# Conversion work queued behind a slot's other work on ScalarE, and w_out split by the second block

## The chip, the cores and the metric

The kernel runs on one core of one Trainium2 chip. The metric is the device time of one execution in microseconds; the time of a kernel is the median of several runs. TensorE (PE) does the matmuls, VectorE (DVE), ScalarE (ACT) and GpSimd (POOL) the element work, and SyncE (SP) only issues DMAs. Each engine takes its instructions in the order in which the program lists them, so an instruction that waits holds up all that stands behind it on its engine.

## The reference

Pooled attention feeds a dense layer pair, and its result a routed layer with eight experts, of which each token takes one:

```python
k_p = k.reshape(B, H, Sp, pool, D).mean(axis=3)          # B=8, H=8, Sp=72, pool=8, D=64
v_p = v.reshape(B, H, Sp, pool, D).mean(axis=3)
attn = softmax(scale * np.matmul(q, k_p.transpose(0, 1, 3, 2)))
x = np.matmul(attn, v_p)                                   # 4608 tokens x 512
h = x @ w_in                                               # 512 x 2048
g = np.where(h >= 1, h, np.where(h <= -1, 0.0, (h + 1) ** 2 / 4))
x = g @ w_out                                              # 2048 x 512
expert = argmax(x @ w_gate, axis=1)                        # 8 experts
out = gate_w * (np.maximum(x @ w1[expert], 0.0) @ w2[expert])
```

All data is float32.

## The kernel before

The 4608 tokens are 36 tiles of 128, in ten blocks (3, then 4 each, then 3 and 2 tiles). Each block runs 16 steps, one for each chunk of 128 hidden units. In step m, `f1` multiplies chunk m+2 of w_in with the block's x (12 matmuls), and `f2` multiplies chunk m's activations with chunk m of w_out (3 matmuls a tile). Every float32 product is made of three matmuls on operands split into a high and a low part; the high part is a ScalarE copy, the low part a subtraction (`low_part`, line 266, on GpSimd for weights).

Between `f1` and `f2`, and again after `f2`, stands a slot: an even one and an odd one in each step. Slots carry the attention of the next block's tiles as units: `u_qt` (transposes q, line 384 and its ScalarE copy 386), `u_sc_all` (scores, line 327; reductions 334 and 336 on VectorE; the exponential, line 341, on ScalarE), `u_turn_p` and `u_place_p` (probabilities turned through DRAM: transposes 414 and 416, store to `p_d` line 417, load into `PT` line 423), `u_pv` (line 443, copies 449 and 450). Units come round about every three steps in the first block.

The first block (`j == 0`, here from about 30 to 150 us) also prepares the weights. Each weight chunk is loaded raw (`load_raw`, SP queue) and goes through `tick`, one tick a slot: `convert_a` is two ScalarE passes (lines 545 and 549, the second writes `SGN`, a part of tile `WG`); `convert_b` queues two VectorE passes in `pend` (line 557, which reads the raw words and `SGN` and writes a PSUM bank, and line 560, which finishes the chunk `dst`); `mix` takes work from `pend`. Two ticks later `convert_c` makes the high part on ScalarE (line 571) and the low part on GpSimd (line 266). Chunks of w_in stay in `W`. Chunks of w_out go into one of four slots of `WO`, and the first block also stores their high and low parts to `wo_d` in DRAM (line 574, 512 KB a chunk), from where all later blocks load them (`load_out`, line 611, ScalarE queue).

`f1`'s own element work is a chain over two engines: line 626 (VectorE), 627 (ScalarE), 631 (VectorE, in `larger`), 632 (ScalarE, `larger`), 266 (VectorE, `lower`). `larger`, `lower` and some parts of units go into the list `later`, which `flush` empties once in a slot, in the order in which they were put in. Each `f1` writes PSUM bank 0 or 1 by turns. The score and transpose units share two more banks in the first block.

The lines that set the order in a slot of the first block are `tick()`, then the units, then `flush()`; `tick(late)` either calls `convert_a` and `convert_b` at once or appends them to `later`. After a block, `route_steps` finds each token's expert in small steps, one or two a slot, with a number of pauses between (`wait`).

Of the kernel before, what the change touches and what calls it, by code (L numbers as in the profile page):

```python
# [8 lines left out]
F32 = mybir.dt.float32  # L9
# [4 lines left out]
ACTF = mybir.ActivationFunctionType  # L14
# [10 lines left out]
def attention_ffn_routed_experts_kernel(  # L25
# [12 lines left out]
    nc = tc.nc  # L38
    B, H, S, D = q.shape
    NT, DM = out.shape  # L40
# [5 lines left out]
    KF = DFF // 128  # L46
# [16 lines left out]
    NB = len(blocks)  # L63
# [7 lines left out]
    dram = ctx.enter_context(tc.tile_pool(name="dram", bufs=1, space=bass.MemoryType.DRAM))  # L71

    wo_d = dram.tile([KF, 128, 2, DM], F32R, name="wo_d")
    yrow_d = dram.tile([NT + 128, ROW], F32, name="yrow_d")
    perm_d = dram.tile([128 * NE * NTILE, 1], I32, name="perm_d")
    perm_t = perm_d.rearrange("(p e r) o -> p (e r o)", p=128, e=NE)
# [7 lines left out]
    def r32(ap):  # L84
        return ap.bitcast(F32)
# [3 lines left out]
    WO = sb.tile([128, 4, 2, DM], F32R, name="WO")  # L89
# [17 lines left out]
    def fx(o, n):  # L107
        return FX[:, o:o + n]
# [24 lines left out]
    WOF = [fx(512 + 512 * i, 512) for i in range(4)]  # L133
# [5 lines left out]
    def wi(m, lo, c):  # L139
        o = m * 1024 + lo * 512 + c * 128  # L140
        return W[:, o:o + 128]

    def wi4(m, lo):
        o = m * 1024 + lo * 512
        return W[:, o:o + 512]
# [119 lines left out]
    def low_part(lo, x, hi, eng=nc.gpsimd):  # L265
        eng.tensor_tensor(out=lo, in0=x, in1=r32(hi), op=ALU.subtract)  # L266
# [3 lines left out]
    def mix(n=1):  # L270
        for _ in range(min(n, len(pend))):
            pend.popleft()()
# [3 lines left out]
    def flush():  # L276
        for _ in range(len(later)):
            later.popleft()()
# [257 lines left out]
    def cvt_dst(i):  # L536
        m, o = order[i]
        return (WOF[m % 4] if o else DFI[m % 3]), RB[i % NRB].rearrange(
            "p a (x w) -> p a x w", w=2)
# [23 lines left out]
    def convert_ab(i):  # L563
        convert_a(i)
        convert_b(i)

    def convert_c(i):
        m, o = order[i]
        dst, _ = cvt_dst(i)
        hi, lo = (WO[:, m % 4, 0], WO[:, m % 4, 1]) if o else (wi4(m, 0), wi4(m, 1))  # L570
        nc.scalar.activation(out=hi, in_=dst, func=ACTF.Copy)  # L571
        low_part(lo, dst, hi)
        if o:
            nc.sync.dma_start(out=r32(wo_d[m]), in_=r32(WO[:, m % 4]))


    FIRST, MORE = AHEAD + 2, 1
# [12 lines left out]
    def more_raw(i):  # L590
        if i < len(order) and order[i]:
            load_raw(*order[i], i % NRB)

    def tick(late=False):

        n = ticks[0]
        mix(4)
        if n > 0:
            more_raw(n - 1 + NRB)
        if 0 <= n - 2 < len(order) and n != 3:  # L600
            convert_c(n - 2)
        if n < len(order):
            if late:
                later.append(lambda: convert_ab(n))
            else:
                convert_ab(n)
        ticks[0] += 1

    def load_out(g):

        nc.scalar.dma_start(out=r32(WO[:, g % 4]), in_=r32(wo_d[g % KF]))

    def f1(j, m):
        g = j * KF + m
        n = blocks[j][1] * 128
        o = ps[m % 2][:, 0:n]
        for c in range(KD):
            xh, xl = XT[:, j % 2, 0, c, 0:n], XT[:, j % 2, 1, c, 0:n]
            nc.tensor.matmul(o, wi(m, 0, c), xh, start=(c == 0), stop=False)  # L619
            nc.tensor.matmul(o, wi(m, 0, c), xl, start=False, stop=False)  # L620
            nc.tensor.matmul(o, wi(m, 1, c), xh, start=False, stop=(c == KD - 1))  # L621
        r = (JK if j == 0 and m % 2 else FR)[:, 0:n]
        gh, gl = FG[:, g % (AHEAD + 1), 0, 0:n], FG[:, g % (AHEAD + 1), 1, 0:n]


        nc.vector.tensor_scalar(r, o, -1.0, 1.0, op0=ALU.max, op1=ALU.min)  # L626
        nc.scalar.activation(out=r, in_=r, func=ACTF.Square, scale=0.5, bias=half)  # L627
        mix()

        def larger():  # L630
            nc.vector.tensor_tensor(out=o, in0=r, in1=o, op=ALU.max)  # L631
            nc.scalar.activation(out=gh, in_=o, func=ACTF.Copy)  # L632
            if KF <= g + 1 < len(steps):
                load_out(g + 1)
            later.append(lower)

        def lower():
            low_part(gl, o, gh, nc.vector)
        later.append(larger)
# [26 lines left out]
    def route_steps(j, bk):  # L666
# [22 lines left out]
            nc.tensor.matmul(pb[:, 0:n * 32], PICK4, LT[:, 0:n * 32], start=True, stop=True)  # L689
            V.transpose(out=LGT[:, 0:n].rearrange("p t x -> p (t x)"), in_=pb[:, 0:n * 32])  # L690

        wait = 2 if j < NB - 2 else 1
        for t in range(n):
            st.append(lambda t=t: turn(t))
            st.extend([pause] * wait)
# [107 lines left out]
    def pick_first():  # L803
        V = nc.vector
        cnt = CB[:, 0]
        mx, mn = MX4[:, 0], MN4[:, 0]
        g = G1[:, 0]
        V.tensor_reduce(out=mx, in_=cnt, axis=AX.X, op=ALU.max)
        V.tensor_scalar(g, cnt, mx, None, op0=ALU.is_equal)
        V.scalar_tensor_tensor(out=g, in0=g, scalar=-16.0, in1=iota4[:, 0], op0=ALU.mult,  # L810
                               op1=ALU.add)
        V.tensor_reduce(out=mn, in_=g, axis=AX.X, op=ALU.min)
        V.tensor_scalar(FST, g, mn, None, op0=ALU.is_equal)
        V.tensor_scalar(FSI, mn, 16.0, None, op0=ALU.add)
        V.tensor_copy(FSR, FSI)

        V.tensor_scalar(POS0, FSI, -float(CAP), -float(EARLY * 128), op0=ALU.mult, op1=ALU.add)
        for t in range(LN):
            V.tensor_scalar(IDF[:, t:t + 1], pcol, float((blocks[-1][0] + t) * 128 - NT), None,
                            op0=ALU.add)  # L820
# [4 lines left out]
    def fetch_first(dst, t0, n):  # L825
        r = nc.values_load(FSR[0:1, 0:1], engines=[SP], min_val=0, max_val=NE - 1)
        nc.sync.dma_start(out=dst, in_=tiles_of[:, bass.ds(r, 1), t0:t0 + n].rearrange(
            "p o r -> p (o r)"))
# [5 lines left out]
    def load_first(i):  # L834
        if not first:
            first.append(nc.values_load(FSR[0:1, 0:1], engines=[ACT], min_val=0, max_val=NE - 1))
        src = (w1, w2)[i // 4][bass.ds(first[0], 1)].rearrange("o (c p) f -> p (o c) f", p=128)

        if i < 4:
            nc.scalar.dma_start(out=ST1[:, i:i + 1], in_=src[:, i:i + 1])  # L840
        else:
            nc.scalar.dma_start(out=ST2[:, 2 * i - 8:2 * i - 6], in_=src[:, 2 * i - 8:2 * i - 6])
# [129 lines left out]
    def q_gather(qn, i):  # L972
        gather(XG[i], q_ids(qn, i), qn == 0)
# [158 lines left out]
    with tc.manual_schedule():  # L1132
# [9 lines left out]
        def run_units(n):  # L1142
            for _ in range(n):
                units.popleft()[1]()
            if qloads:
                qloads.popleft()()
# [64 lines left out]
        steps = [(j, m) for j in range(NB) for m in range(KF)]  # L1211
# [14 lines left out]
        def slot(j, s):  # L1226

            want = min(state["units"], -(-(s + 1) * state["units"] // (22 if j == NB - 2 else 29 - 2 * AHEAD + 2)))
            wide[0] = False
            if j == 0:  # L1230
                for _ in range(min(1, PER[s // 2]) if s % 2 == 0 else PER[s // 2] - 1):
                    tick()
            run_units(want - state["done"])
            state["done"] = max(want, state["done"])
            flush()
            if j == 0 and kv:
                kv.popleft()()
            for _ in range(2 if j >= NB - 2 else 0 if wide[0] else 1 + s % 2):
                if todo:
                    todo.popleft()()  # L1240
            if j == PICK + 2 and s == 0:
                pick_first()
            for i in range(8):
                if 32 * (j - NB + 2) + s == LF[i]:
                    load_first(i)
            if j == NB - 2:

                if s == 1:
                    fetch_first(IDA, 0, EARLY)
                if s == 9:  # L1250
                    for i in range(EARLY):
                        q_gather(0, i)
            if j == NB - 1:
                if s == 3:
                    nc.gpsimd.iota(IO, pattern=[[1, 128]], base=0, channel_multiplier=0,
                                   allow_small_or_imprecise_dtypes=True)
                if s == 17:
                    fetch_first(IDQ, EARLY, 4 * NQ)
                if s == 27:
                    nc.vector.tensor_copy(IDMF, IDQ)  # L1260
                if s in CV1:
                    cvt1(CV1.index(s))
                if s in QT0:
                    q_tx(0, QT0.index(s))
                if s in (25, 27):
                    cvt2(0, (s - 25) // 2)

        for m in range(AHEAD):
            f1(0, m)
            flush()  # L1270
            while ticks[0] < CAHEAD + 2 + m:
                tick()
                flush()
        for g, (j, m) in enumerate(steps):
            if m == 0:
# [222 lines left out]
```

## Time and profile before

| | us |
|---|---|
| median of 3 runs | 1396.14 (1395.46 to 1397.46) |
| the profiled execution | 1394.67 |
| its span in the trace | 1393.0 |
| PE busy | 1353.9 (97%) |
| DVE / ACT / POOL busy | 762.4 / 433.3 / 355.5 |

The time of the profiled execution is 1.67 us more than its span, and 1.47 us less than the median. A busy PE says little by itself; what matters is where it stands idle, and behind whom.

### The profile page before, as it was taken

The page shows a single profiled execution, that of the slowest core. Times are in us where ns is not written, and L with a number is a line of the kernel's source. Part 1 is how long each engine was busy: PE and PEld are TensorE (multiplying, and loading weights), DVE is VectorE, ACT ScalarE, POOL GpSimd, SP SyncE. Part 2 cuts the span into 40 slices and gives each one's busy share as a digit, 9 for nine tenths or more (in the row PEclk, how much of TensorE's full clock was granted, in tenths as well). Part 3 has the DMA queues.
Part 4 walks back from the last instruction along what each step waited for, and adds up shares of the span by engine and source line. Part 5 has one row for each costly group of instructions (what it writes and reads, how often), then busy time and mean ns, then how long its engine had stood idle before and what let it go on. Part 6 is the DMA issues. An engine that isn't in the chain of part 4 may idle for free. (4 is left out here: it accounts for less than half of the span.)

```text
span 1393.0 us, 22129 instructions
## 1 busy us (share of the span) xinstructions
PE 1353.9 (97%) x8114; PEld 1111.7 (80%) x8114; DVE 762.4 (55%) x1539; ACT 433.3 (31%) x730; POOL 355.5 (26%) x517
## 2 busy tenths in 40 slices
PE   7788999999999999999999999999999999999998
PEld 6666778888778788788788788889878888888886
DVE  5698566656666675566666556455532323323426
ACT  5667232222222222222222233343121111111335
POOL 4475636004304203313310011021231211111211
PEclk9899999999999999999999999999999999999999
DMA  9986656546637555555453344572543223331235
GB/s 235 287 274 221 186 144 193 144 123 176 179 116 197 149 161 155 159 166 150 148 158 111 111 142 146 187 264 79 182 137 107 92 72 109 104 107 59 86 125 188
DMA packets 170702, 213.48 MB, mean 153 GB/s; under 512 B 83431, under 2 KB 114439, under 8 KB 170568
## 3 DMA queue, kind: packets, MB, share of 16 engines
q1 hardware_dynamic: 135992, 102.29, 25.7%
q10 hardware_dynamic: 26784, 88.16, 18.9%
q0 software_dynamic: 7792, 21.35, 4.7%
q8 instruction: 71, 1.16, 0.4%
q14 instruction: 63, 0.52, 0.1%
HBM read 188.30 MB, written 47.03 MB: 169 GB/s over the span
## 5 line engine op out<-in xcount | busy, mean ns | idle before, releaser
L619 PE MATMUL ps<-XT,W 128*128 128x512 f32 (+2 forms) x640 | 243.3, 380 | 5.3 <-ACT W L571 2.4
L621 PE MATMUL ps<-XT,W 128*128 128x512 f32 (+2 forms) x640 | 237.6, 371 | 2.2 <-POOL W L266 2.2
L620 PE MATMUL ps<-XT,W 128*128 128x512 f32 (+2 forms) x640 | 237.6, 371 | 0.5 <-DVE XT L450 0.5
L647 PE MATMUL ps<-WO,FG 128*128 128x512 f32 x576 | 231.2, 401 | 1.0 <-ACT Y L656 1.0
L648 PE MATMUL ps<-WO,FG 128*128 128x512 f32 x576 | 225.9, 392 | 0.0
L649 PE MATMUL ps<-WO,FG 128*128 128x512 f32 x576 | 225.3, 391 | 0.0
L627 ACT ACTIVATE FX<-FX,half 128x512 f32<-128x512 f32 (+2 forms) x152 | 104.0, 684 | 379.7 <-DVE FX L626 357.9
L626 DVE TENSOR_SCALAR FX<-ps 128x512 f32<-128x512 f32 (+2 forms) x152 | 96.9, 638 | 122.0 <-PE ps L621 121.5
L619 PEld LDWEIGHTS ps<-XT,W 128*128 128x128 f32 x640 | 121.3, 190 | 30.4 <-ACT W L571 3.6
L745 POOL DMA_INDIRECT perm_d<-idt,POSI x36 | 35.2, 978 | 424.3 <-DVE SM L731 357.5
L621 PEld LDWEIGHTS ps<-XT,W 128*128 128x128 f32 x640 | 121.3, 190 | 21.4 <-POOL W L266 3.4
L1019 DVE SCALAR_TENSOR_TENSOR FG<-ps,FG 128x512 fp32r<-128x512 f32 (+1 forms) x64 | 43.2, 674 | 173.3 <-ACT FG L1018 173.3
L631 DVE TENSOR_TENSOR ps<-FX,ps 128x512 f32<-128x512 f32 (+2 forms) x152 | 97.6, 642 | 73.5 <-ACT FX L627 73.5
L620 PEld LDWEIGHTS ps<-XT,W 128*128 128x128 f32 x640 | 121.4, 190 | 18.4 <-DVE XT L450 1.1
L647 PEld LDWEIGHTS ps<-WO,FG 128*128 128x128 f32 x576 | 108.4, 188 | 25.7 <-issue 2.8
L632 ACT ACTIVATE FG<-ps 128x512 fp32r<-128x512 f32 (+2 forms) x160 | 88.8, 555 | 125.4 <-DVE ps L631 116.8
L649 PEld LDWEIGHTS ps<-WO,FG 128*128 128x128 f32 x576 | 108.6, 188 | 23.5
L266 DVE TENSOR_TENSOR FG<-ps,FG 128x512 fp32r<-128x512 f32 (+2 forms) x160 | 100.8, 630 | 44.6 <-ACT FG L632 43.1
L648 PEld LDWEIGHTS ps<-WO,FG 128*128 128x128 f32 x576 | 108.6, 188 | 19.8
L1018 ACT ACTIVATE FG<-ps 128x512 fp32r<-128x512 f32 (+1 forms) x64 | 37.4, 584 | 244.1 <-PE ps L1015 230.5
L254 POOL TENSOR_TENSOR AT<-AT 72x256 f32<-72x256 f32 x104 | 79.2, 762 | 128.9 <-DMA AT<-in_v_dram 67.7
L1013 PE MATMUL ps<-XT,W 128*128 128x512 f32 (+1 forms) x256 | 99.0, 387 | 2.9 <-ACT XT L997 2.5
(235 smaller groups left out, 2157.8 us busy)
## 6 DMA issues: line engine op xcount, KB each, us to landing
WO<-wo_d ACTq DMA_DIRECT2D x144, 512.0 KB
AT<-in_moe_w_dram SPq DMA_DIRECT2D x30, 1024.0 KB
p_d<-AT SPq DMA_DIRECT2D x29, 384.0 KB
AT<-in_v_dram SPq DMA_DIRECT2D x59, 144.0 KB
wo_d<-WO SPq DMA_DIRECT2D x16, 512.0 KB
AT<-in_k_dram SPq DMA_DIRECT2D x56, 144.0 KB
PT<-p_d SPq DMA_DIRECT2D x58, 128.0 KB
yrow_d<-Y ACTq DMA_DIRECT2D x7, 1032.0 KB
```

Source lines behind the costliest of these rows:

```text
L266: eng.tensor_tensor(out=lo, in0=x, in1=r32(hi), op=ALU.subtract)
L619: nc.tensor.matmul(o, wi(m, 0, c), xh, start=(c == 0), stop=False)
L620: nc.tensor.matmul(o, wi(m, 0, c), xl, start=False, stop=False)
L621: nc.tensor.matmul(o, wi(m, 1, c), xh, start=False, stop=(c == KD - 1))
L626: nc.vector.tensor_scalar(r, o, -1.0, 1.0, op0=ALU.max, op1=ALU.min)
L627: nc.scalar.activation(out=r, in_=r, func=ACTF.Square, scale=0.5, bias=half)
L631: nc.vector.tensor_tensor(out=o, in0=r, in1=o, op=ALU.max)
L632: nc.scalar.activation(out=gh, in_=o, func=ACTF.Copy)
L647: nc.tensor.matmul(o, gh, WO[:, g % 4, 0], start=(m == 0), stop=False)
L648: nc.tensor.matmul(o, gh, WO[:, g % 4, 1], start=False, stop=False)
L649: nc.tensor.matmul(o, gl, WO[:, g % 4, 0], start=False, stop=(m == KF - 1))
L1013: nc.tensor.matmul(o, e1(0)[:, c, ms], xh, start=(c == 0), stop=False)
```

## The change

In the first block every `tick` is now called with `late`, so that `convert_a` and `convert_b` of a chunk stand in `later` behind `larger`. The w_out chunk is stored unsplit into a new DRAM tile `wf_d` (256 KB a chunk), straight from `dst`. The second block's `f1` calls `split_out`: it loads a chunk of `wf_d` two steps ahead into `WOF`, splits it on ScalarE and GpSimd into `WO` as the first block does, and stores the parts to `wo_d` for the blocks after it. `route_steps` of block 0 leaves three pauses between its steps where it left two.

```diff
+    wf_d = dram.tile([KF, 128, DM], F32, name="wf_d")
...
         if o:
-            nc.sync.dma_start(out=r32(wo_d[m]), in_=r32(WO[:, m % 4]))
+            nc.sync.dma_start(out=wf_d[m], in_=dst)
...
+    def split_out(g):
+
+        if g < 2 * KF - 2:
+            nc.scalar.dma_start(out=WOF[(g + 2) % 4], in_=wf_d[(g + 2) % KF])
+        if g >= KF:
+            hi, lo = WO[:, g % 4, 0], WO[:, g % 4, 1]
+            nc.scalar.activation(out=hi, in_=WOF[g % 4], func=ACTF.Copy)
+            low_part(lo, WOF[g % 4], hi)
+            nc.sync.dma_start(out=r32(wo_d[g % KF]), in_=r32(WO[:, g % 4]))
...
-            if KF <= g + 1 < len(steps):
+            if KF <= g + 3 <= 2 * KF + 1:
+                split_out(g + 1)
+            elif 2 * KF < g + 2 <= len(steps):
                 load_out(g + 1)
...
-        wait = 2 if j < NB - 2 else 1
+        wait = 3 if j == 0 else 2 if j < NB - 2 else 1
...
                 for _ in range(min(1, PER[s // 2]) if s % 2 == 0 else PER[s // 2] - 1):
-                    tick()
+                    tick(True)
...
             while ticks[0] < CAHEAD + 2 + m:
-                tick()
+                tick(True)
```

The lines of the changed kernel stand one lower than before up to 574, and eleven lower from 611 to 660: 545 is 546, 549 is 550, 571 is 572, but 626 is 637, 631 is 642 and 632 is 643.

ScalarE, in a step of the first block whose even slot holds scores. `FG` is the high part of the activations (`larger`), `Y` holds raw words, `WG` the sign words, `W` and `WO` the split weights. Before:

```order
L571 ACTIVATE WO<-FX 128x512
L545 ACTIVATE FX<-Y 128x512
L549 ACTIVATE WG<-Y 128x512
L632 ACTIVATE FG<-ps_72 128x384
L341 ACTIVATE AT<-AT 128x8x72
L571 ACTIVATE W<-FX 128x512
L545 ACTIVATE FX<-Y 128x512
L549 ACTIVATE WG<-Y 128x512
```

The same place in the changed kernel:

```order
L572 ACTIVATE WO<-FX 128x512
L643 ACTIVATE FG<-ps_73 128x384
L546 ACTIVATE FX<-Y 128x512
L550 ACTIVATE WG<-Y 128x512
L342 ACTIVATE AT<-AT 128x8x72
L572 ACTIVATE W<-FX 128x512
L546 ACTIVATE FX<-Y 128x512
L550 ACTIVATE WG<-Y 128x512
```

The two passes of `convert_a` moved from ahead of `larger`'s copy to behind it; the exponential and the copy of the next w_in chunk now stand behind them.

VectorE in the same slot and the start of the next. `ps_77` (`ps_78` in the change) is the PSUM bank that line 557 writes. Before:

```order
L334 TENSOR_REDUCE smx_124<-ps_78 128x4
L336 TENSOR_TENSOR AT<-ps_78,smx_124 128x4x72
L334 TENSOR_REDUCE smx_124<-ps_79 128x4
L557 SCALAR_TENSOR_TENSOR ps_77<-Y,WG 128x512
L336 TENSOR_TENSOR AT<-ps_79,smx_124 128x4x72
L631 TENSOR_TENSOR ps_73<-AT,ps_73 128x384
L560 SCALAR_TENSOR_TENSOR FX<-FX,ps_77 128x512
L266 TENSOR_TENSOR FG<-ps_73,FG 128x384
```

The same place in the changed kernel:

```order
L335 TENSOR_REDUCE smx_125<-ps_79 128x4
L337 TENSOR_TENSOR AT<-ps_79,smx_125 128x4x72
L335 TENSOR_REDUCE smx_125<-ps_80 128x4
L337 TENSOR_TENSOR AT<-ps_80,smx_125 128x4x72
L642 TENSOR_TENSOR ps_74<-AT,ps_74 128x384
L558 SCALAR_TENSOR_TENSOR ps_78<-Y,WG 128x512
L561 SCALAR_TENSOR_TENSOR FX<-FX,ps_78 128x512
L267 TENSOR_TENSOR FG<-ps_74,FG 128x384
```

Line 557 left the place between the score reductions and stands now directly behind `larger`'s maximum (631, now 642). In the even slots without scores it stood there already.

SyncE's DMA issues at the start of the second block. Before:

```order
L1308 DMA perm_d<-AT 128x288
L1222 DMA WG<-in_moe_w_gate_dram 32x16x8 x4
L245 DMA AT<-in_v_dram 72x512 x2
L229 DMA AT<-in_q_dram 32x9x32 x4
L245 DMA AT<-in_v_dram 72x512
L229 DMA AT<-in_q_dram 32x9x32 x4
```

The same place in the changed kernel:

```order
L622 DMA wo_d<-WO 128x1024 x2
L1321 DMA perm_d<-AT 128x288
L622 DMA wo_d<-WO 128x1024
L1235 DMA WG<-in_moe_w_gate_dram 32x16x8 x4
L246 DMA AT<-in_v_dram 72x512 x2
L230 DMA AT<-in_q_dram 32x9x32 x4
L622 DMA wo_d<-WO 128x1024
L246 DMA AT<-in_v_dram 72x512
L230 DMA AT<-in_q_dram 32x9x32 x4
```

A store of a split chunk, which waits for GpSimd's low part, now stands among the loads of q and v.

## Rows read from the trace of the kernel before

**Rows 1.** The profile's page, its head.

```profile
span 1393.0 us, 22129 instructions
```

**Rows 2.** Stretches: start:end, length, busy PE, PEld, DVE, ACT, POOL, clock, DMA share.

```profile
64.00:124.00 60.00, 49.68 (x361) 40.62 (x359) 54.15 (x88) 43.78 (x79) 40.44 (x44) 0.94 0.86 283
153.00:247.00 94.00, 94.00 (x609) 75.40 (x610) 54.23 (x108) 27.82 (x47) 43.25 (x82) 1.00 0.61 172
93.00:99.00 6.00, 4.26 (x31) 3.58 (x31) 5.09 (x10) 6.00 (x13) 5.84 (x7) 0.72 0.67 215
```

**Rows 3.** TensorE's waits from 64 to 140 us: us in total, times, longest.

```profile
PE ps L443 <- DMA PT<-p_d: 5.1, 3, 2.5
PE ps L619 <- ACT W L571: 2.4, 3, 1.2
PE ps L621 <- POOL W L266: 2.2, 3, 0.8
PE ps L384 <- DVE AT L336: 1.8, 3, 1.0
```

**Rows 4.** Timeline of VectorE, 109 to 117 us: start, length, instruction, [idle before].

```profile
109.50 0.69 DVE L557 SCALAR_TENSOR_TENSOR ps<-Y,WG 128x512 int32<-128x512 int32 x1
110.09 0.45 DVE L336 TENSOR_TENSOR AT<-ps,smx 128x288 f32<-128x288 f32 x1
110.46 0.56 DVE L631 TENSOR_TENSOR ps<-FX,ps 128x384 f32<-128x384 f32 x1
110.92 0.68 DVE L560 SCALAR_TENSOR_TENSOR FX<-FX,ps 128x512 int32<-128x512 int32 x1
...
116.18 1.27 DVE L557 SCALAR_TENSOR_TENSOR ps<-AT,WG 128x512 int32<-128x512 int32 x1 [0.26 <-ACT WG L549]
```

**Rows 5.** Timeline of ScalarE, 111 to 117 us.

```profile
111.11 0.49 ACT L632 ACTIVATE FG<-ps 128x384 fp32r<-128x384 f32 x1 [2.79 <-DVE ps L631]
111.50 0.68 ACT L341 ACTIVATE AT<-AT 128x576 f32<-128x576 f32 x1
112.07 0.62 ACT L571 ACTIVATE W<-FX 128x512 fp32r<-128x512 f32 x1
112.59 0.66 ACT L545 ACTIVATE FX<-Y 128x512 f32<-128x512 f32 x1
113.14 0.78 ACT L549 ACTIVATE WG<-Y 128x512 f16<-128x512 f32 x1
113.78 0.60 ACT L627 ACTIVATE AT<-AT,half 128x384 f32<-128x384 f32 x1
...
115.99 0.59 ACT L386 ACTIVATE AT<-ps 128x512 f32<-128x512 f32 x1
```

**Rows 6.** Groups of VectorE instructions, 64 to 124 us: busy, mean ns, idle before.

```profile
L557 DVE SCALAR_TENSOR_TENSOR ps<-WG 128x512 int32<-128x512 int32 x9 | 11.3, 1256 | 0.5 <-ACT WG L549 0.4
L557 DVE SCALAR_TENSOR_TENSOR ps<-Y,WG 128x512 int32<-128x512 int32 x6 | 5.4, 898 | 0.7 <-ACT WG L549 0.7
L557 DVE SCALAR_TENSOR_TENSOR ps<-AT,WG 128x512 int32<-128x512 int32 x3 | 2.7, 900 | 1.0 <-ACT WG L549 1.0
L450 DVE SCALAR_TENSOR_TENSOR XT<-ps,XT 128x512 fp32r<-128x512 f32 x3 | 2.1, 690 | 2.4 <-ACT XT L449 2.4
```

**Rows 7.** Timeline of all engines around 98.6 us, VectorE's and GpSimd's rows.

```profile
98.58 3.17 DVE L557 SCALAR_TENSOR_TENSOR ps<-WG 128x512 int32<-128x512 int32 x1 [0.18 <-ACT WG L549]
99.90 1.29 POOL L266 TENSOR_TENSOR WO<-FX,WO 128x512 fp32r<-128x512 f32 x1
```

**Rows 8.** Timeline of GpSimd at 112.8 us.

```profile
112.77 1.29 POOL L266 TENSOR_TENSOR W<-FX,W 128x512 fp32r<-128x512 f32 x1 [4.34 <-ACT W L571]
```

**Rows 9.** Waits of SP's queue, 36 to 140 us: us in total, times, longest.

```profile
SPq L574 <- POOL WO L266: 22.7, 13, 6.0
```

**Rows 10.** Instructions on tile WO, 140 to 250 us, and VectorE's timeline at 169.6 us.

```profile
L611 ACTq DMA_DIRECT2D WO<-wo_d x19: 326/326/362, 139.8 to 249.4; - x19
...
169.59 0.71 DVE L376 STREAM_TRANSPOSE AT<-AT 128x512 f32<-128x512 f32 x1 [3.29 <-DMA AT<-in_q_dram]
```

## The prediction

> **What bounds the kernel now.** I read first where TensorE stands idle, since the span of 1393.0 us [rows 1] is its queue. In the second block it is busy for the whole of 94 us [rows 2], so an engine behind it there may get slower at no cost as long as it is not late. The first block is different: from 64 to 124 us TensorE is busy 49.7 of 60 us while VectorE is busy 54.2 [rows 2]. So I asked whom TensorE waits for there [rows 3]: turned probabilities from DRAM (5.1 us), high and low parts of a w_in chunk (2.4 and 2.2), score reductions (1.8), together 11.5 us. The timelines show what stands behind the last three. The w_in copy (571, at 112.07) is the third of an unbroken run on ScalarE that had waited 2.79 us for VectorE's 631 [rows 5]; 631 comes straight after the reductions, with a pass of line 557 between them [rows 4]. VectorE is the slow one. Part of its time is no work: 18 passes of line 557 took 11.3 + 5.4 + 2.7 = 19.4 us [rows 6], where one takes 0.69 when nothing disturbs it [rows 4], 12.4 in all. So 7.0 us are stretches. The longest, 3.17 us, ended at 101.75, 0.56 us behind the end of a GpSimd low part [rows 7]. The Trainium skill, SBUF — State Buffer, section Who interferes with whom, says that a VectorE instruction with two SBUF inputs and a GpSimd instruction that reads SBUF lock each other out for a whole instruction; this trace agrees.
>
> **The change, part by part.** All of it lies in the first block but the splitting.
>
> *The two ScalarE passes behind `larger`.* In the changed order 550 stands behind 643, which needs 642; and 558, which needs 550, is VectorE's next instruction after 642. What ran side by side becomes a chain. Its length by rows of before: 631 to 632, 111.11 − 110.46 = 0.65; 632, 111.50 − 111.11 = 0.39; 545, 113.14 − 112.59 = 0.55; 549, 0.78 [rows 4, 5]. So 558 starts 2.4 us after 642 started, where the instruction behind 631 started after 110.92 − 110.46 = 0.46: 1.9 us in which VectorE stands still. In a step with `u_qt` line 557 already waits 0.26 for 549 [rows 4]; 386 (0.59) and 632 (0.39) now go first [rows 5], about 1.2 us in all. 64 to 124 us holds nine steps, three of them of that kind: 6 × 1.9 + 3 × 1.2 = +15.0 us of VectorE's time. Behind it are the rest of the conversions, the sums of the softmax and the next score reductions; TensorE waits for these.
>
> *What VectorE gets back.* The 0.4 + 0.7 + 1.0 = 2.1 us in which 557 waited for 549 [rows 6] are inside the new waits. It also waited 2.4 us at line 450 for a copy that hung on the late probabilities [rows 6]; an engine that comes later finds it done. And the stretches: 558 now starts when 550 ends, the moment at which ScalarE starts the next instruction, at the earliest a 572. GpSimd's low part starts 112.77 − 112.07 = 0.70 after a 571 [rows 5, 8], and 558 is done after 0.69. They would just miss each other, so I take all 7.0 us as gained; the other end is 0. By the page's rule whoever starts first holds the port, so a small shift brings the stretches back: with them the sum below is 7.0 worse. Net: 15.0 − 2.1 − 2.4 − 7.0 = +3.5 us.
>
> *The last wait for a w_in chunk.* What is late in the first block stays late, because TensorE has no slack after it. The last of the three waits counted under line 571 belongs to a fourth step with scores. There 557 leaves the reductions, so 631 comes 110.09 − 109.50 = 0.59 earlier [rows 4], but 545 and 549 now stand ahead of the exponential and of 571: 113.78 − 112.59 = 1.19 later [rows 5]. +0.6. The first load of `split_out` is also issued there, 0.33 on ScalarE [rows 10]: +0.9 together.
>
> *Stores of 256 KB instead of 512.* SP waited 22.7 us for GpSimd before stores to `wo_d` [rows 9]; the new store waits for `dst`, which is done earlier. Loads and the turned probabilities behind it go out sooner, and 4 MB fewer are written. This can take away TensorE's 5.1 us for `PT` [rows 3]. I count nothing of it further, because TensorE then meets VectorE's lateness at the same places: those 5.1 us lie between waits that VectorE sets. Its other end, the whole 5.1, is in the first rival.
>
> *The second block.* 16 copies (0.62 each, as 571 [rows 5]) and 16 low parts (1.29 [rows 8]) go to engines that are busy 27.8 and 43.3 of 94 us [rows 2]; hidden by TensorE's own work, with about three steps between a split and its `f2`. Each store waits for GpSimd with loads of q and v behind it. VectorE already waited 3.29 us for q there [rows 10] without an idle TensorE. One step is 94/16 = 5.9 us, so a lateness of a few us is covered; 0 to +3 us, and I take 0. The longer pauses of the router move small work within the block: nothing.
>
> *The clock.* Where TensorE paused in 93 to 99 us the granted clock was 0.72 [rows 2], so 1.2 GHz for 56% of 6 us and 1.7 us of work lost. More pauses can bring another such stretch, partly hidden by waits: 0 to +3.4, and I take +0.6. The Trainium skill, TensorE: Matmul & The Clock Gate, section What's actually happening, has the throttled state as the default that activity releases; by it the higher end is nearer, 3 us slower than my sum.
>
> **Sum.** +3.5 + 0.9 + 0.6 = +5.0 us. On the profiled execution's 1394.67 that is 1399.7; the median of the runs lies 1.47 us higher, so I predict 1401 us, 0.36% slower. About 0.2% (2.8 us) is what a measurement of this kernel can tell from no change.
>
> **The rivals.**
> - *VectorE gains, faster.* The change wins if the new standstill is below (2.1 + 2.4 + 7.0) / 9 = 1.28 us a step on average; mine is 15.0 / 9 = 1.67. It can be lower if 642 is ready later than 550 for another reason, so that the chain overlaps a wait that is there anyway. Then TensorE also gets the earlier `PT`, and ends up to 5.1 us earlier: 1391. For it speak SP's 22.7 us; against it that 558 stands right behind 642 in nine of nine steps.
> - *Even.* The standstill is near 1.3 us, and half of the stretches go: within 2.8 us of 1396, say 1397.
> - *The stretches stay, slower by more.* GpSimd's share of work is unchanged and its rows fill 40.4 of 60 us [rows 2]; if 558 meets it at other places, the 7.0 us are not gained: 1401 + 7 = 1408.
> - *The second block stalls.* q or v comes so late behind a store that VectorE holds up `f1`'s chain by more than its slack: +3 on top, 1404.
>
> **Chances.** My forecast 0.40, stretches stay or the second block stalls 0.19, even 0.17, faster 0.24. Slower by over 0.2% is 0.40 + 0.19 = 0.59. The range that leaves out 2 in 10 goes from 1391 (the full gain of `PT`) to 1408; the forecast's own range is 1399 to 1404.
>
> **What would show it.** Right: line 558 waits for 550 by 1 to 2 us in nearly every step; no pass of it is much longer than 0.7; TensorE waits longer for score reductions and for the w_in copy; its waits for `PT` shrink; the second block still has no idle TensorE. Wrong: VectorE is no busier in waiting than before and TensorE's idle time from 64 to 140 us falls below 11.5 us; or the first block ends as before and the loss sits in the second, behind q, `PT` or a split chunk of w_out.

## The result, and the profile after

The changed kernel takes 1409.01 us (median of five runs, 1407.34 to 1419.76) against 1396.14 (five runs, 1392.58 to 1397.46). The ratio on record is 1.0116, 95% interval 1.0096 to 1.0136. It is not the quotient of the two medians, which is 1.0092; the ratios in brackets below are of the same kind, and differences in us are between medians. It is slower, as forecast, but by 13 us where 5 were forecast, and 1 us beyond the range. The execution that was profiled is the slowest of the five (1419.76); its waits are read below, its lengths are not used for the sums.

Of the lines read below, 557 is now 558, 560 is 561, 266 is 267, 336 is 337, 376 is 377, and `f1`'s matmuls 619 to 621 are 630 to 632. In some experiments they lie one to six lines further on.

The head of the page, which answers to [rows 1]:

```profile
span 1418.0 us, 22193 instructions
```

Stretches in the columns of [rows 2]: the middle of the first block, a piece near its end, two pieces inside the second block, and the second block.

```profile
64.00:124.00 60.00, 45.60 (x361) 37.81 (x358) 44.59 (x80) 38.85 (x71) 36.47 (x42) 0.97 0.80 242
140.00:153.00 13.00, 9.92 (x45) 8.11 (x44) 7.93 (x16) 7.93 (x14) 9.87 (x14) 0.70 0.46 117
190.00:195.00 5.00, 1.98 (x7) 1.33 (x6) 3.24 (x6) 2.26 (x5) 2.71 (x4) 0.81 0.51 149
195.00:200.00 5.00, 5.00 (x15) 3.79 (x15) 2.70 (x4) 1.48 (x4) 2.82 (x5) 0.51 0.70 170
167.00:271.00 104.00, 100.98 (x629) 80.32 (x628) 59.72 (x115) 35.93 (x62) 65.24 (x107) 0.97 0.67 190
```

Beside [rows 2] two things differ. From 64 to 124 us VectorE, which filled 54 of 60 us, now fills 44.6, and TensorE is busy 4 us less (45.6 against 49.7): VectorE does not work more, it stands. And the second block, whose TensorE was never idle, now has 3.0 us without work, behind which the granted clock is 0.51, the lower level (1.2 GHz), for 5 us.

TensorE's waits from 28 to 330 us (us in total, times, longest):

```profile
PE ps L630 <- DVE FG L267: 15.6, 8, 3.0
PE ps L385 <- DVE AT L337: 5.5, 4, 2.4
PE ps L444 <- DMA PT<-p_d: 4.2, 3, 1.6
PE ps L328 <- ACT AT L387: 2.8, 1, 2.8
PE ps L328 <- ACT AT L289: 1.8, 1, 1.8
```

The stretch of [rows 3] is shorter, 64 to 140 us. The kernel before has the same rows from 28 to 330 us, and two more above 1.5 us:

```profile
PE ps L327 <- ACT AT L386: 3.9, 1, 3.9
PE ps L619 <- DVE FG L266: 1.9, 1, 1.9
```

The waits for W copies and W low parts are gone from the list. In their place stands one that came once before, with 1.9 us, and now comes eight times: the first matmul of `f1` waits for 267, `lower`, the last reader of the PSUM bank that it writes. Score reductions (337) cost 5.5 where they cost 1.8.

Where `lower` is held up is seen in the timeline around 97 us (start, length, engine, line; in brackets the idle time before):

```profile
95.62 0.65 ACT L546 ACTIVATE FX<-Y 128x512 f32<-128x512 f32 x1
96.17 0.76 ACT L550 ACTIVATE WG<-Y 128x512 f16<-128x512 f32 x1
96.97 0.70 DVE L558 SCALAR_TENSOR_TENSOR ps<-Y,WG 128x512 int32<-128x512 int32 x1 [1.82 <-ACT WG L550]
97.70 0.69 DVE L561 SCALAR_TENSOR_TENSOR FX<-FX,ps 128x512 int32<-128x512 int32 x1
...
98.30 0.55 DVE L267 TENSOR_TENSOR FG<-ps,FG 128x384 fp32r<-128x384 f32 x1
...
99.00 0.41 PE L630 MATMUL ps<-XT,W 128*128 128x384 f32 x1 [2.42 <-DVE FG L267]
```

VectorE stands 1.82 us for ScalarE's 550, runs 558 and 561, and only then 267, for which TensorE stands 2.42 us. This is the standstill of the prediction, at the price that it gave (1.9). From 28 to 150 us, the whole of the first block's conversions, VectorE's groups of this line and its wait read as follows (busy, mean ns, idle before; the wait: us, times, longest). First the kernel before:

```profile
L557 DVE SCALAR_TENSOR_TENSOR ps<-WG 128x512 int32<-128x512 int32 x15 | 15.5, 1032 | 1.7 <-ACT WG L549 1.6
L557 DVE SCALAR_TENSOR_TENSOR ps<-Y,WG 128x512 int32<-128x512 int32 x10 | 8.2, 818 | 1.0 <-ACT WG L549 1.0
L557 DVE SCALAR_TENSOR_TENSOR ps<-AT,WG 128x512 int32<-128x512 int32 x5 | 4.1, 820 | 2.5 <-ACT WG L549 2.5
```

```profile
DVE ps L557 <- ACT WG L549: 5.1, 13, 1.1
```

And the changed kernel:

```profile
L558 DVE SCALAR_TENSOR_TENSOR ps<-WG 128x512 int32<-128x512 int32 x15 | 11.1, 741 | 7.9 <-ACT WG L550 7.9
L558 DVE SCALAR_TENSOR_TENSOR ps<-Y,WG 128x512 int32<-128x512 int32 x10 | 8.5, 850 | 7.7 <-ACT WG L550 7.7
L558 DVE SCALAR_TENSOR_TENSOR ps<-AT,WG 128x512 int32<-128x512 int32 x5 | 3.5, 700 | 8.2 <-ACT WG L550 8.2
```

```profile
DVE ps L558 <- ACT WG L550: 23.9, 15, 2.3
```

The stretches shrink: 15.5 + 8.2 + 4.1 = 27.8 us of busy time become 11.1 + 8.5 + 3.5 = 23.1, 4.7 less. The wait grows by 23.9 − 5.1 = 18.8. `after_q` (below), which has the same code there and was profiled near its median (1404.59 against 1404.43), waits 23.9 us there too.

The second block's loss starts at a transpose of q, the one of [rows 10] that waited 3.29 us:

```profile
189.45 0.71 DVE L377 STREAM_TRANSPOSE AT<-AT 128x512 f32<-128x512 f32 x1 [7.72 <-DMA AT<-in_q_dram]
...
193.03 0.68 DVE L267 TENSOR_TENSOR FG<-ps,FG 128x512 fp32r<-128x512 f32 x1
...
193.76 0.79 PE L630 MATMUL ps<-XT,W 128*128 128x512 f32 x1 [3.02 <-DVE FG L267]
```

The same chain as in the first block: what VectorE waits for stands ahead of `lower`, and TensorE finds its bank taken.

### The profile page after: what moved, and what is told of

Read it like the earlier page. It is cut to its first block, busy times and chain, and to the rows that moved or that the text cites. A ratio compares the mean times of both kernels' runs of the same rounds, so it can differ in the third digit from the quotient of the medians.

```text
span 1418.0 us, 22193 instructions
## 1 busy us (share of the span) xinstructions
PE 1366.3 (96%) x8114; PEld 1120.9 (79%) x8114; DVE 760.1 (54%) x1539; ACT 443.5 (31%) x746; POOL 374.2 (26%) x533
## 5 line engine op out<-in xcount | busy, mean ns | idle before, releaser
L630 PEld LDWEIGHTS ps<-XT,W 128*128 128x128 f32 x640 | 122.8, 192 | 42.8 <-ACT FX L546 10.7
L632 PEld LDWEIGHTS ps<-XT,W 128*128 128x128 f32 x640 | 122.7, 192 | 18.8 <-POOL W L267 0.2
L631 PEld LDWEIGHTS ps<-XT,W 128*128 128x128 f32 x640 | 122.8, 192 | 17.9 <-DVE XT L451 0.5
L642 DVE TENSOR_TENSOR ps<-FX,ps 128x512 f32<-128x512 f32 (+2 forms) x152 | 97.5, 642 | 72.7 <-ACT FX L638 72.7
L255 POOL TENSOR_TENSOR AT<-AT 72x256 f32<-72x256 f32 x104 | 77.5, 745 | 104.3 <-DMA AT<-in_v_dram 60.6
```

## The experiments

Times are medians; "before" is the kernel before, run beside each on the same chip (1394.67 to 1395.32 us). "First block" is from the first `f1` matmul to the first copy of `evict_y`, "second block" from there to the next such copy, both in the profiled execution: 123.0 and 97.5 us in the kernel before. One profile tells such a length to 2 or 3 us: kernels whose first blocks are the same code differ there by 1.9 (`before_q`, 124.9) and 2.4 (`split_only` and `s_q_first`, 120.3 and 122.7).

**One part alone.** `late_only` is the kernel before with the late passes:

```diff
-                    tick()
+                    tick(True)
...
-                tick()
+                tick(True)
```

> The kernel before with the conversion passes behind the slot's other work alone; w_out is stored split in the first block as before. Theory A (VectorE's line 557 waits for 549 in each step, and the release of f1's PSUM bank by line 266 stands behind it): most of the 12.9 us of loss, 1404 to 1407 us, TensorE waiting 10 us or more for line 266 in the first block. Theory B (the loss sits in the second block, behind the split and its stores): 1396 to 1399 us, and no wait for 266 above 3 us.

`split_only` is the changed kernel with these two edits turned round.

> The changed kernel with the conversion passes back ahead of the slot's other work; w_out still stored unsplit, split and stored by the second block, with the router's longer pauses. Theory A: 1396 to 1400 us, the first block no longer than before. Theory B: 1403 us or more. If the smaller stores of the first block help, it is below 1394.

`late_only` takes 1404.42 us (1.0067, 1.0052 to 1.0081): 9.1 us more than before, with 131.0 in the first block (+8.0) and 98.6 in the second. `split_only` takes 1399.62 (1.0034, 1.0017 to 1.0051): 4.3 more, with 120.3 in the first and 102.5 in the second (+5.0). 9.1 + 4.3 = 13.4 is about the loss of the whole change, 12.9: two losses, one a block, from two parts that share no line. The eight blocks behind take the same to within 2 us in all fourteen profiles; what comes after them differs by up to 3 us, which was not followed. TensorE's waits in the first block of `late_only`, 28 to 152 us:

```profile
PE ps L619 <- DVE FG L266: 11.4, 7, 2.4
PE ps L384 <- DVE AT L336: 5.5, 4, 2.7
PE ps L443 <- DMA PT<-p_d: 5.4, 3, 2.2
```

They are the changed kernel's; all waits of this block add up to 27.5 us, against 19.6 in the kernel before. In its second block TensorE waits for nothing.

**The bank, or VectorE's time?** `lower_first` is the changed kernel in which `larger` of the first block calls `lower` at once, so that 267 stands ahead of 558.

```diff
-            later.append(lower)
+            if j:
+                later.append(lower)
+            else:
+                lower()
```

> The changed kernel, with the low part of the activations (line 267, which releases f1's PSUM bank) directly behind the maximum and its copy, ahead of the conversion of the chunk. Theory A1 (the loss of the first block goes through the bank): TensorE's 12.6 us of waits for 267 in the first block fall below 4, 1399 to 1403 us. Theory A2 (VectorE's lost time alone counts, whatever stands behind the wait): the waits move to the score reductions and the w_in copies, 1406 to 1409 us.

1409.19 us (1.0092, 1.0076 to 1.0109): no gain that can be told, since the interval overlaps the changed kernel's. VectorE's waits from 28 to 150 us:

```profile
DVE FG L267 <- ACT FG L643: 9.1, 16, 0.6
DVE ps L558 <- ACT WG L550: 8.6, 12, 1.1
```

The standstill is divided over two lines, 9.1 + 8.6 = 17.7 us. TensorE's wait for 267 in the first block is down from 12.6 to 1.0 us, but the copies (572) and low parts of w_in take its place with 4.8 and 4.0. So the bank is only the place at which TensorE meets a late VectorE.

`late_b` takes the standstill away and leaves VectorE's order as changed: ScalarE's two passes run at once, only 558 and 561 are put into `later`.

```diff
-                later.append(lambda: convert_ab(n))
+                convert_a(n)
+                later.append(lambda: convert_b(n))
```

> The changed kernel, but ScalarE prepares each chunk at once, as before, and only the two VectorE passes (558, 561) stay behind the slot's other work; VectorE's order is then the changed kernel's row for row. Theory S (the first block's loss is the standstill of 558 behind ScalarE's pass 550, and what queues behind it): the waits of 1.8 us go, PE's waits for line 267 with them, and the first block is back at about 120 to 123 us (135 in the changed kernel, 120.4 with at-once passes and the unsplit store), total 1398 to 1401 with the second block's loss of about 5 left in. Theory O (VectorE's order is the cause: 267 behind 558 and 561, wherever ScalarE stands): the waits for 267 stay at 10 us or more and the total at 1406 to 1410.

1400.74 us (1.0045, 1.0032 to 1.0058), 8.3 less than the changed kernel; first block 119.7. VectorE's instructions there are the changed kernel's, in the same order. Its wait for 550 and TensorE's for 267, 28 to 150 and 28 to 152 us:

```profile
DVE ps L558 <- ACT WG L550: 1.1, 3, 0.4
...
PE ps L631 <- DVE FG L267: 3.1, 4, 1.8
```

Theory S holds: the first block's loss is the standstill. All kernels without it have first blocks of 119.7 to 124.9 us, those with it 128.6 to 131.3 (135.3 in the changed kernel's profiled execution). The stretches are back in `late_b` (14.0 + 10.4 + 5.4 = 29.8 us for line 558) and cost it nothing that shows.

**Why q comes late.** The first guess was that SP waits for GpSimd's low part before each split store. `store_later` issues each store one step later, when the low part is long done.

```diff
+    def store_out(g):
+        nc.sync.dma_start(out=r32(wo_d[g % KF]), in_=r32(WO[:, g % 4]))
...
-            nc.sync.dma_start(out=r32(wo_d[g % KF]), in_=r32(WO[:, g % 4]))
+            if g > KF:
+                store_out(g - 1)
+            if g == 2 * KF - 1:
+                later.append(lambda: store_out(g))
```

> The changed kernel, with each store of a split chunk issued one step later, so that SP seldom waits for GpSimd before loads of q and v. If the second block's loss is SP's queue behind those stores: VectorE's wait for q falls from 7.7 to about 3.3 us, TensorE's wait of 3.0 us goes, 1404 to 1406 us. If it is the traffic of the 8 MB of stores: q stays as late, 1408 to 1410 us.

1410.9 us (1.011, 1.0092 to 1.0127), the q wait 7.31: that guess fell. SP's waits around the block's start show what took the place of the wait for low parts. First the changed kernel from 155 to 190 us, then `store_later` from 150 to 184:

```profile
SPq L622 <- POOL WO L267: 8.5, 3, 4.9
SPq L246 <- POOL AT L257: 2.9, 2, 2.0
...
SPq L1235 <- POOL WG L1230: 0.2, 1, 0.2
```

```profile
SPq L246 <- POOL AT L257: 6.4, 4, 2.3
...
SPq L1241 <- POOL WG L1236: 2.7, 1, 2.7
...
SPq L615 <- POOL WO L267: 0.9, 1, 0.9
```

The stores' wait is gone but for 0.9 us, and of the 7.6 us less, 6.0 come back at the loads of v (246) and of the router's weights (1235, now 1241), which also wait for GpSimd and stand ahead of q. Three kernels on `split_only`, all with its three pauses and its split, then took the stores out of SP's way or the q loads ahead of them.

`s_both8`: the first block also stores the first eight chunks split, and the second block leaves these eight stores out.

```diff
             nc.sync.dma_start(out=wf_d[m], in_=dst)
+            if m < 8:
+                nc.sync.dma_start(out=r32(wo_d[m]), in_=r32(WO[:, m % 4]))
...
+            if g >= KF + 8:
```

> The kernel with at-once passes; the first eight chunks are stored split by the first block too, and the second block leaves out the stores of these eight (it still loads and splits all sixteen). Nothing is left out of the result. If the stores are what makes q late (theory Q or T), the q wait falls to about 3 us and the second block to about 98 us (102.5); the first block carries 256 KB more a chunk and gives back up to 2.6 us; total 1395 to 1398. If the split on ScalarE and GpSimd or the three pauses make it late, the q wait stays at 6 to 7 us and the total at 1399 to 1402.

`s_store_act`: the stores one step later and from ScalarE's queue (`nc.scalar.dma_start` in `store_out`).

> The kernel with at-once passes; the split stores are issued by ScalarE one step later instead of by SP, the same bytes on another queue. Theory Q (order in SP's queue): q comes 17 us after the block's start as before, its wait falls to about 3, total about 1394 to 1396. Theory T (the bytes): q comes at 20 us or later, total 1398 to 1401; the loads of the unsplit chunks then share ScalarE's queue with the stores and may come late themselves, which would show as a wait of line 621 for WOF.

`s_q_first`: two batches of q loads a slot.

```diff
-            if qloads:
+            for _ in range(min(2, len(qloads))):
                 qloads.popleft()()
```

> The kernel with at-once passes (1399.6, 7 us late in the second block), with the q loads of the second block issued two batches a slot instead of one, so that they stand ahead of more of the split stores in SP's queue. Theory Q (the q batches stand behind 512 KB stores in the queue and are late only by that): the first q transpose comes about 17 us after the block's start (21.7 there), its wait falls from 6.8 to about 3, the stretch at 1.2 GHz after it goes, and the total is about 1394 to 1396. Theory T (the DMA engines are full with the block's 256 KB loads and 512 KB stores, whatever the order): q comes at 20 us or later and the total stays at 1398 to 1401.

They take 1398.53 (1.0032, 1.0019 to 1.0046), 1397.64 (1.0018, 1.0009 to 1.0028) and 1395.71 us (1.0006, 0.9997 to 1.0015). `s_q_first` writes and reads every byte that `split_only` does, and is level with the kernel before: the order decides, not the bytes. In `s_both8` the second block is as well mended (98.5), but its total lies 2.8 us above `s_q_first`'s; its first block is the longer one (124.4), and what the stores in both forms cost there was not followed further. SP's q batches, first in `split_only`, then in `s_q_first`, with the transpose that takes them:

```profile
155.44 2.57 SPq L230 DMA_DIRECT2D AT<-in_q_dram  x4
158.42 0.34 SPq L622 DMA_DIRECT2D wo_d<-WO  x1
...
166.37 2.29 SPq L230 DMA_DIRECT2D AT<-in_q_dram  x4
...
170.28 0.71 DVE L377 STREAM_TRANSPOSE AT<-AT 128x512 f32<-128x512 f32 x1 [6.81 <-DMA AT<-in_q_dram]
```

```profile
158.36 4.66 SPq L230 DMA_DIRECT2D AT<-in_q_dram  x8
...
164.01 4.55 SPq L230 DMA_DIRECT2D AT<-in_q_dram  x8
...
170.17 0.71 DVE L377 STREAM_TRANSPOSE AT<-AT 128x512 f32<-128x512 f32 x1 [3.79 <-DMA AT<-in_q_dram]
```

The transpose starts 170.28 − 168.66 = 1.6 us after the end of the fourth batch's issue in the one, 170.17 − 168.56 = 1.6 in the other, and 1.5 to 1.6 in the kernel before and the changed one too. So what is late is the issue on SP, not the transfer. In `split_only` SP waited 5.7 us for low parts ahead of 622 from 140 to 170 us, with the loads behind it. The Trainium skill, DMA: Bandwidth & Descriptors, section Anatomy of one DMA — SWDGE (gpsimd) path, says that a DMA's semaphore wait is done by the issuing sequencer before dispatch; it tells this for DMAs of GpSimd, and the trace shows the same of SP.

One more place stands in that queue: the router's weights (`gate_weights`), whose loads wait for a GpSimd memset that comes behind the split's low parts (3.2 us in `s_store_act`, 0.2 in the kernel before). First the kernel before, whose second block starts at 152.33 us, then `split_only`, where it starts at 148.59:

```profile
146.16 2.02 SPq L1222 DMA_DIRECT2D WG<-in_moe_w_gate_dram  x4
```

```profile
150.55 2.66 SPq L1235 DMA_DIRECT2D WG<-in_moe_w_gate_dram  x4
```

They go out 6.2 us ahead of the block in the one and 2.0 behind its start in the other, and 2.0 behind it in `store_later`, `s_store_act`, `s_both8` and `s_q_first` too: SP waits for GpSimd there, with the stores or without them. `s_gate_later` is `split_only` with that call two steps later.

```diff
-                    gate_weights()
...
             slot(j, 2 * m)
+            if (j, m) == (1, 2):
+                gate_weights()
```

> The kernel with at-once passes and the split (1399.6; first q batch issued 9.4 us after the block's start, 6.1 in the kernel before; fourth 20.1 against 15.7). The loads of the router's weights, which stand ahead of the q loads in SP's queue and wait for a GpSimd memset that the split's low parts push back, are issued two steps later, behind the first q loads. Theory G (half of q's lateness is this place in the queue): the first batch is out by about 7 us, the fourth by about 17 to 18, the q wait is 4 to 5 us, TensorE no longer waits for line 267 in the second block, total 1395 to 1397. Theory N (only the stores between the batches matter): the fourth batch stays at 19 us or later and the total at 1398 to 1401.

1398.08 us (1.002, 1.0011 to 1.003): between the theories. The first batch is out 7.0 us after the block's start, as theory G has it, the fourth 18.2. So moving those loads gives back 21.7 − 20.0 = 1.7 us of the 4.4 that q was late in `split_only`, and taking the stores from SP's queue 1.9 to 3.1 (`s_store_act` and `s_both8` below). The two are no clean division, because each wait takes the place of the other. By the rows of SP, 3.3 of the 4.4 us are lost before the end of the first batch (9.4 us after the block's start against 6.1), the rest between the batches.

Eleven of the kernels together, by their timelines: start of the second block, start of the q transpose, the difference, and TensorE's wait for line 267 (266) in the second block.

```
before        152.33  169.59  17.3   0
s_both8       152.67  171.23  18.6   0
s_q_first     151.50  170.17  18.7   0
after_q       159.38  178.18  18.8   0
s_store_act   150.16  169.95  19.8   0.2
s_gate_later  150.12  170.11  20.0   0.4
split_only    148.59  170.28  21.7   2.1
late_b        151.04  172.78  21.7   2.2
store_later   161.35  183.54  22.2   2.6
lower_first   157.04  179.38  22.3   2.8
after         166.85  189.45  22.6   3.0
```

The last column is the third less 19.6, to within 0.1, wherever that is positive; the three kernels left out (15.3, 17.1 and 19.2) have no such wait. By this the kernel before had 19.6 − 17.3 = 2.3 us to spare.

**Are the two losses separate, and do the repairs win anything?** `after_q` is the changed kernel with two q batches a slot, `late_b_q` is `late_b` with them, `before_q` the kernel before with them.

> The changed kernel with two batches of q loads a slot, the late passes kept. If the two losses are separate (first block: the standstill; second block: the place of the q loads in SP's queue), this takes back 4 us as it did with at-once passes: 1404 to 1406, first block still 130 us or more, no PE wait for line 267 in the second block. If the second block's loss is fed by the late passes too, it stays at 1408 to 1410.

> The changed kernel with both repairs: ScalarE's passes at once, only VectorE's behind the slot's other work, and two batches of q loads a slot. Both repairs together give 1395 to 1397, level with the kernel before within its 0.2%: then the unsplit store and the place of the VectorE passes are worth nothing by themselves. A gain (1393 or less) would speak for the VectorE passes behind the scores, which the changed kernel hid under the standstill.

> A control: the kernel before with two batches of q loads a slot. If this order repairs only what the split stores push back, it stays at 1394 to 1396. If it is a gain of its own (the q wait of 3.29 us there goes and PE feels it), it gives 1391 to 1393, and the 4 us that it gave the kernel with the split are not all the split's loss.

They take 1404.43 (1.0072, 1.0051 to 1.0092), 1396.22 (1.0007, 0.9993 to 1.0021) and 1394.22 us (0.9996, 0.9983 to 1.0009). The q order gives back 4.6 us in the changed kernel, 4.5 in `late_b`, 3.9 in `split_only`, and nothing in the kernel before, though the q wait goes there too. Taking away the standstill gives 8.3 without the q order and 8.2 with it. So the losses add, both are found, and no kernel here beats the kernel before by more than can be measured.

## Why the prediction came out as it did

- **The standstill.** Right in mechanism, place and price: forecast 15.0 us for 64 to 124 us at 1.9 or 1.2 a step, found 8 × 1.8 = 14.4 there. The 1.2 for steps with `u_qt` was wrong: all eight are 1.77 to 1.82. Wrong above all was the sum's end at 124 us. Passes of the line go on to 147, and those outside the stretch wait 23.9 − 14.4 = 9.5 us, 3.0 before; 5.5 of the 6.5 more come behind 124. The term "15.0 − 2.1 = 12.9" measured 18.8 over the block. This is the first step that failed: a stretch chosen to read the bound was used as the whole place of the cost.
- **What VectorE gets back.** Forecast 7.0 from the stretches and 2.4 at line 450. Found 4.7 and 1.6 (line 451 waits 3.6 us from 28 to 150 where it waited 5.2 before). What the prediction drew from the shared port came out: of the 15 passes that waited for 550, 14 run in 0.70 us, and what is left of the stretches lies in passes that come without a wait, as the 1.45 us one at 100.10.
- **So VectorE's net** is 18.8 − 4.7 − 1.6 = +12.5, not +3.5, and TensorE paid about 8 us of it in the first block (`late_only`, whose own net by the same three terms is 17.2 − 4.4 − 1.8 = +11.0). That it pays for most of VectorE's loss was right. Which waits grow was half right: score reductions did, the W copies did not; the prediction did not name `lower`, which stands behind 558 and frees the bank. `lower_first` shows that this left the size alone.
- **The last W wait, +0.9:** that wait has no row in the changed kernel; TensorE now stands for 267 instead, so the +0.9 has nothing that it could be read from.
- **Stores of 256 KB, not counted:** right. TensorE's wait for `PT` is 5.4 us in `late_only`, 4.2 in the changed kernel. `split_only`'s first block is 2.6 us shorter than before's, but `s_q_first`, with the same code there, has 122.7; no gain is shown.
- **The second block, 0:** the second step that failed. "A lateness of a few us is covered", from a step of 5.9 us, was too much: 2.3 us were to spare, and q came 4.4 to 5.3 us later. The rival described this mechanism (q behind a store, VectorE holds up `f1`) and priced it at +3; the measured price is 3.9 to 4.6, about 2 to 3 of it TensorE's wait, and in some executions a stretch at the lower clock behind it. The store was only a part of it: the prediction did not count that the split's low parts also push GpSimd's memset back, and with it the router's loads ahead of q.
- **The clock, +0.6:** not separable in the first block. The changed kernel's piece from 140 to 153 us at 0.70 lies among TensorE's waits, so part of it is hidden. In the second block, TensorE of `split_only` stood 2.1 us and was granted 0.66 from 175 to 180 us; that of `late_b` stood 2.2 us and was granted 1.00 from 170 to 200. Their second blocks are 102.5 and 101.0 us, and 5 × (1 − 0.66) = 1.7 us of work is about the 1.5 between them. The other profiles with such a wait go the same two ways: in `lower_first` the clock stays at 1.00 and the second block is 101.5, in `store_later` and the changed kernel it falls, and they are 104.3 and 104.7. Against the 98.9 to 99.0 of the kernels with two q batches a slot, the first kind is longer by its wait alone (2.1 and 2.6, for waits of 2.2 and 2.8). Why the clock fell in three and not in two stays open.

The forecast's +5.0 stands against 9.1 for the late passes and 4.3 for the split. "Stretches stay", the rival that gave 1408, came near by accident: the stretches mostly went.

## What to carry to other kernels

When a stretch of the profile shows the bound, count the change's instructions over the whole program before multiplying; here 5.5 us of the wait lay just behind the window. An order change that puts a producer behind another engine's chain costs its consumer a standstill, and moving a third instruction ahead of it only moves the place where it is felt. How much lateness an engine can take is not a step's length: read how long a wait it already has there without effect, and who issues what it waits for.

## What was not expected of the hardware

A load's lateness can come wholly from the queue that issues it: with equal bytes, q moved by 3.0 us relative to the block (21.7 to 18.7) when 16 small loads were issued with one store and two loads of v less between them. And SP spends 0.46 us (1.84 for four) to 0.58 (4.66 for eight) on each of these loads of 36 KB, more than on a store of 512 KB (0.34). Sixteen of them are 7 to 9 of the 13.2 us from the first batch's start to the fourth's end in `split_only`, and q was there 1.6 us later, so that the pace of SP's queue, not of moving, set when q was there.
